# Streaming the folded w_in of a fused attention and two-MoE kernel past the packed values of all batches

## The chip, the cores and the metric

The kernel runs on one core of one Trainium2 chip. The metric is device time in microseconds (us): the median over the runs that are shown. Engines are called by name: TensorE (PE in the profile, PEld its weight loads), VectorE (DVE), ScalarE (ACT), GpSimd (POOL), SyncE (SP, which only issues DMAs here).

## The reference

```python
# q, k, v: (8 batches, 8 heads, 576, 64); p: (8, 8, 32, 64)
def sm_attn(qq, kk, vv):
    s = scale * np.matmul(qq, kk.transpose(0, 1, 3, 2))
    s = s - np.max(s, axis=-1, keepdims=True)
    a = np.exp(s)
    a = a / (np.sum(a, axis=-1, keepdims=True) + 1e-09)
    return np.matmul(a, vv)
p_packed = sm_attn(p, k, v)              # 32 packed rows for each head
out = sm_attn(q, p_packed, p_packed)
# heads side by side: x is (4608 tokens, 512)
def moe(x, w_in, w_out):                 # w_in (512, 2048), w_out (2048, 512)
    h = x @ w_in
    return (h * np.cos(h)) @ w_out
def moe2(x, w_in, w_out, a, b):          # the same sizes, g a ratio of polynomials in h
    ...
    return (g @ w_out).astype(np.float32)
```

The MoE weights arrive as 64-bit floats.

## The kernel before

**Precision.** A matmul of float32 accuracy is made of three matmuls on values that are split in a high part, rounded to the format that TensorE takes (F32R), and a low part, the rest: high x high, high x low, low x high (`PASSES`). `split` (lines 65 to 67) makes the high part with a copy on ScalarE and the low part with a subtraction on VectorE or GpSimd, as its caller says. `convert` (lines 74 to 93) turns a 64-bit weight chunk of 128 x 512 into the two parts: four operations on VectorE, three on ScalarE, two on GpSimd.

**W'.** The second attention ends in a product with p_packed and is followed by the product with w_in of the first MoE. The kernel multiplies p_packed by w_in first. For each batch this is W', 8 heads x 32 rows = 256 rows of 2048 columns, kept as two groups (`G`) of 128 rows. Then h = a W', where a is the second attention's softmax.

**First stage.** A loop over n = 0 to 16 (lines 386 to 412), one step for each batch and group of four heads, packs p: scores (`s1`), exponential, transposes (`et`), product with v (`pv`), transpose and split of the packed p (`ppt`). In its first steps three chunks of w_in a step are converted (line 402), all of w_in is kept in SBUF as high and low parts, and the second attention of batch 0 (`attn2_steps`) goes along, a step at a time. As soon as two batches (a pair P) are packed, the 16 units of their W' join a list, and each step works off four. A unit (`wunit`, lines 267 to 292) is three matmuls of 512 columns, a copy from PSUM (on ScalarE, every fourth on VectorE) into a tile `wev`, of which there are three, and, after every second unit, two stores to HBM of 256 KB each, issued by ScalarE.

**Between the stages.** A loop over the 16 chunks of w_out (lines 574 to 583) converts them, works off the last 16 units, and loads W' of batch 0 back (`load_wq`, four tiles of 512 columns) and splits it, the low part on GpSimd.

**First MoE.** 128 slots (`slots`, line 593), for 8 batches x 2 halves of the tokens x 8 pairs of blocks of 128 hidden columns. A slot makes h with 12 matmuls (`mm_h`), then the chain to g = h cos(h) (`chain1`), then, two slots late, y with 24 matmuls (`mm_y`, the sum over the pairs stays in PSUM). Two buffers in PSUM hold h. The chain reduces h to a cosine's range: ScalarE makes h/(2 pi) + 1/4, VectorE rounds it to a whole number and takes 2 pi times that from h, ScalarE takes the sine, VectorE multiplies by h. Between a batch's slots stand the next batch's second attention (every second slot), its loads and splits of W', and the conversions of the second MoE's weights (one in three slots, from slot 16 on).

**Second MoE.** 144 slots of 512 tokens x 128 hidden columns, 24 matmuls of 512 columns each.

**Order.** The program is written out without loops at run time. The framework orders each engine's instructions by the program's order and its own model of when they are ready, and adds the semaphores; each engine works off its queue in order. `hold` fixes single places of that order.

Of the kernel before, what the change touches and what calls it, by code (L numbers as in the profile page):

```python
# [20 lines left out]
def pack_attention_moe_moe_kernel(  # L21
# [76 lines left out]
    wd = [dram.tile([G, 128, DFF], F32, name=f"wd{b}") for b in range(B)]  # L98
# [11 lines left out]
    if True:  # L110
# [5 lines left out]
        e0, e0a = ExitStack(), ExitStack()  # L116
# [3 lines left out]
        ps0 = e0.enter_context(tc.tile_pool(name="ps0", bufs=1, space=PSUM))  # L120

        w1i_s = [[wb_p.tile([128, DFF], F32R, tag="wb", bufs=8, name="w1i") for x in range(2)] for i in range(NKD)]
# [33 lines left out]
        nc.vector.memset(coef[:, 6:7], 0.25)  # L156
# [92 lines left out]
        def ppt(n):  # L249
            b, g = divmod(n, G)  # L250
            P, b2 = divmod(b, 2)
            if P not in wl_t:
                wl_t[P] = tuple(
                    wi_p.tile([128, H // 2, 2, 64], F32R, tag=f"wl{i}", bufs=2, name=f"wl{i}") for i in range(2)
                )
# [9 lines left out]
        wev_t = {}  # L265

        def wunit(P, hp, fq):
            ps = ps0.tile([128, 512], F32, tag="w", bufs=2, name="w")
            wl = wl_t[P]
            for i, (a, c) in enumerate(PASSES):  # L270
                nc.tensor.matmul(  # L271
                    out=ps,
                    lhsT=wl[a][:, hp].rearrange("p b m -> p (b m)"),
                    rhs=w1i_s[hp][c][:, 512 * fq:512 * fq + 512],
                    start=(i == 0),
                    stop=(i == 2),
                )
            if fq % 2 == 0:
                wev_t[P, hp] = wi_p.tile([128, 1024], F32, tag="wev", bufs=3, name="wev")
            o = wev_t[P, hp][:, 512 * (fq % 2):512 * (fq % 2) + 512]  # L280
            if fq % 4 == 3:
                nc.vector.tensor_copy(o, ps)
            else:
                nc.scalar.activation(out=o, in_=ps, func=AF.Copy)
            if fq % 2 == 1:
                t = wev_t.pop((P, hp))
                g, gg = divmod(hp, 2)
                for b2 in range(2):
                    nc.scalar.dma_start(
                        out=wd[2 * P + b2][g, 64 * gg:64 * gg + 64, 512 * (fq - 1):512 * (fq + 1)],  # L290
                        in_=t[64 * b2:64 * b2 + 64, :],
                    )

# [3 lines left out]
        def attn2_steps(b, pool, psp, pst, psb, tg, now):  # L297
# [14 lines left out]
            for g in range(G):  # L312
# [12 lines left out]
                sc = psp.tile([128, 2, 512], F32, tag=pst, bufs=psb, name="s2")  # L325
# [17 lines left out]
            for g in range(G):  # L343
# [7 lines left out]
                split(ah, al, aT.rearrange("p c j -> p (c j)"), nc.gpsimd)  # L351
# [14 lines left out]
        cv1 = [(i, j) for i in range(NKD) for j in range(DFF // 512)]  # L366

        def load_w1i(x):
            i, j = cv1[x]
            load_st(x, words(w1i[128 * i:128 * i + 128, 512 * j:512 * j + 512]))  # L370

        def conv_w1i(x):
            i, j = cv1[x]
            c = slice(512 * j, 512 * j + 512)
            convert(w1i_s[i][0][:, c], w1i_s[i][1][:, c], st_t.pop(x), cv_p, 512)
            if x + 2 < len(cv1):
                load_w1i(x + 2)

        prep(0)
        load_w1i(0)  # L380
        load_w1i(1)

        units = []
        tg0 = {"qT": ("kT", 2), "ppT": ("pbd", 2), "aT": ("E", 2)}
        at = attn2_steps(0, wk, ps0, "s1", 1, tg0, lambda: None)
        for n in range(NG + 1):
# [8 lines left out]
            for _ in range(2):  # L395
                if units:
                    wunit(*units.pop(0))
# [7 lines left out]
            for _ in range(2):  # L405
                if units:
                    wunit(*units.pop(0))
# [356 lines left out]
```

## Time and profile before

| | |
|---|---|
| median of 3 runs | 1711.96 us (1711.77 to 1714.64) |
| profiled execution | 1713.67 us |
| its span, first to last instruction | 1711.9 us |
| mean granted clock of TensorE, share of full speed | 0.979 |
| TensorE, weight loads, VectorE, ScalarE, GpSimd busy | 94%, 82%, 81%, 68%, 17% |
| moved by DMA | 183.52 MB |

A row of the profile's lines view reads: line, engine, operation, what is written `<-` what is read (names of tiles), shapes, count | busy time in us, mean ns of one | idle time of the engine just before them, and what ended it. Shapes are partitions x elements. A line can be that of a helper: L67 is the low part of every `split`. Matmuls are pipelined, so TensorE's busy time is not that of an engine at its peak. "Xq" is the sequencer of engine X.

### The profile page before, as it was taken

Reading aid. Unit: us, or ns where it says so; the run is one execution under the profiler, and the core shown is the slowest. Engines: PE = TensorE matmul, PEld = TensorE weight load, DVE = VectorE, ACT = ScalarE, POOL = GpSimd, SP = SyncE. Lnnn points to the kernel's source line nnn. Section 1 sums busy time; section 2 is a strip of 40 time slices with the busy share of each in tenths; the row PEclk is TensorE's granted clock in tenths of the full one; section 3 lists DMA queues with packets and bytes.
Section 4 is the critical chain, followed back from the end, with each engine's and each line's share of the span. In section 5 each row is a group of like instructions: output and inputs, shape, how many; then the busy total and the mean of one; then the engine's idle time right before and its main releaser. Section 6 shows DMA issues by size and latency. Waiting matters only on the chain.

```text
span 1711.9 us, 24200 instructions
## 1 busy us (share of the span) xinstructions
PE 1614.5 (94%) x8832; PEld 1412.0 (82%) x8832; DVE 1382.4 (81%) x2143; ACT 1155.9 (68%) x1885; POOL 298.0 (17%) x203
## 2 busy tenths in 40 slices
PE   5789678999999999999999999999999999999996
PEld 4668478999999999999998888888888888888884
DVE  5893598888888888888658888888888888888884
ACT  3554566565656575756548777877777878787874
POOL 3450552233333332323100000000000000000000
PEclk9989889999999999999999999999999999999998
DMA  9988832443434433434285101001010202020100
GB/s 273 272 254 236 281 104 83 128 135 119 154 122 143 149 135 128 150 120 155 74 274 200 50 25 50 25 27 48 13 62 1 75 0 75 0 74 1 43 7 25
DMA packets 99767, 183.52 MB, mean 107 GB/s; under 512 B 11584, under 2 KB 46400, under 8 KB 99648
## 3 DMA queue, kind: packets, MB, share of 16 engines
q1 hardware_dynamic: 92224, 163.09, 30.0%
q10 hardware_dynamic: 7424, 18.88, 3.7%
q8 instruction: 70, 1.15, 0.3%
q14 instruction: 49, 0.40, 0.1%
HBM read 117.97 MB, written 63.96 MB: 106 GB/s over the span
## 4 chain that ended last, share of the span: by engine, by line
PE 74%; DVE 15%; ACT 4%; issue 3%; DMA 3%; SPq 0%; POOL 0%; ACTq 0%; DVEq 0%; POOLq 0%
PE h L643 23%; PE o L702 23%; PE y L558 14%; PE h L514 7%; PE s L191 3%; DVE gl L67 2%; DVE u L539 2%; DVE g L545 2%; DVE cvp L87 2%; PE w L271 1%; DVE cvp L89 1%; DVE r L540 1%; PE pv L237 1%; DVE cvf L90 1%; DMA st<-in_moe_w_in_dram 1%
## 5 line engine op out<-in xcount | busy, mean ns | idle before, releaser
L558 PE MATMUL y<-gh,w1o 128*128 128x288 f32 x2048 | 433.4, 297 | 0.0
L643 PE MATMUL h<-x,w 128*128 128x512 f32 x1728 | 422.7, 393 | 0.0
L643 PEld LDWEIGHTS h<-x,w 128*128 128x128 f32 x1728 | 324.1, 188 | 74.2
L558 PEld LDWEIGHTS y<-gh,w1o 128*128 128x128 f32 x2048 | 337.9, 189 | 1.4 <-DVE yl L67 0.7
L702 PE MATMUL o<-w,g2h 128*128 128x512 f32 x1152 | 334.0, 394 | 1.3 <-ACT g2h L661 1.3
L558 PE MATMUL y<-gl,w1o 128*128 128x288 f32 x1024 | 298.2, 297 | 8.1 <-DVE gl L67 7.9
L702 PEld LDWEIGHTS o<-w,g2h 128*128 128x128 f32 x1152 | 216.0, 188 | 53.1 <-ACT g2h L661 2.1
L514 PE MATMUL h<-ah,wq 128*128 128x288 f32 x1024 | 232.2, 303 | 26.9 <-DVE g L545 24.9
L558 PEld LDWEIGHTS y<-gl,w1o 128*128 128x128 f32 x1024 | 193.4, 189 | 11.7 <-DVE gl L67 11.3
L514 PEld LDWEIGHTS h<-ah,wq 128*128 128x128 f32 x1024 | 175.2, 192 | 30.4 <-issue 27.4
L702 PE MATMUL o<-w,g2l 128*128 128x512 f32 x576 | 199.8, 393 | 0.0
L677 ACT ACTIVATE sq<-h 128x512 f32<-128x512 f32 x144 | 87.3, 606 | 156.0 <-PE h L643 155.9
L679 DVE SCALAR_TENSOR_TENSOR ab<-sq,coef,ab 128x512 f32<-128x512 f32 x144 | 108.2, 751 | 68.1 <-ACT ab L678 67.9
L514 PE MATMUL h<-al,wq 128*128 128x288 f32 x512 | 153.5, 300 | 0.0
L544 ACT ACTIVATE r<-r,coef 128x576 f32<-128x576 f32 x128 | 99.0, 775 | 70.9 <-DVE r L540 70.1
L538 ACT ACTIVATE u<-h,coef 128x576 f32<-128x576 f32 x128 | 94.2, 736 | 76.1 <-PE h L514 75.4
L91 POOL TENSOR_TENSOR cvf<-cvf,cvs 128x512 f32<-128x512 f32 x64 | 89.6, 1400 | 288.7 <-DVE cvf L90 259.2
L688 DVE SCALAR_TENSOR_TENSOR ab<-ab,y 128x512 f32<-128x512 f32 x144 | 99.5, 691 | 47.8 <-ACT y L685 47.2
L67 DVE TENSOR_TENSOR gl<-g,gh 128x576 fp32r<-128x576 f32 x128 | 117.1, 917 | 18.2 <-ACT gh L66 16.1
L702 PEld LDWEIGHTS o<-w,g2l 128*128 128x128 f32 x576 | 108.0, 188 | 25.6
L680 ACT ACTIVATE c<-h,coef 128x512 f32<-128x512 f32 x144 | 113.8, 790 | 9.8 <-DVE g2l L667 9.8
L545 DVE TENSOR_TENSOR g<-h,r 128x576 f32<-128x576 f32 x128 | 95.9, 750 | 27.4 <-ACT r L544 27.3
(89 smaller groups left out, 2620.7 us busy)
## 6 DMA issues: line engine op xcount, KB each, us to landing
x<-yd SPq DMA_DIRECT2D x36, 512.0 KB
w<-w2d SPq DMA_DIRECT2D x68, 256.0 KB
st<-in_moe_w_in_dram SPq DMA_DIRECT2D x32, 512.0 KB
wd<-wev ACTq DMA_DIRECT2D x64, 256.0 KB
st<-in_moe_w_out_dram SPq DMA_DIRECT2D x32, 512.0 KB
wq<-wd SPq DMA_DIRECT2D x32, 512.0 KB
kx<-in_k_dram SPq DMA_DIRECT2D x16, 576.0 KB
vx<-in_v_dram SPq DMA_DIRECT2D x48, 192.0 KB
```

The costliest lines, as they stand in the source:

```text
L67: lo_eng.tensor_tensor(out=lo, in0=src, in1=hi.bitcast(F32), op=ALU.subtract)
L91: nc.gpsimd.tensor_tensor(out=ff, in0=ff, in1=sg, op=ALU.mult)
L514: last_h[0] = nc.tensor.matmul(out=ps[:, u, 0:HS], lhsT=wq[:, g, a, o:o + 128], rhs=a_t[b, g][c][:, hf * HS:hf * HS + HS], start=(i == 0), ...
L538: nc.scalar.activation(out=u, in_=ph, func=AF.Identity, scale=INV2PI, bias=coef[:, 6:7])
L544: nc.scalar.activation(out=r, in_=r, func=AF.Sin, bias=coef[:, 7:8])
L545: nc.vector.tensor_tensor(out=gt, in0=ph, in1=r, op=ALU.mult)
L558: nc.tensor.matmul(out=y_t[d][:, 0:HS], lhsT=w1o_s[f // 4][a][:, f % 4, 128 * d:128 * d + 128], rhs=gs[c][:, u], start=(f == 0 and i == 0) ...
L643: nc.tensor.matmul(out=ps, lhsT=w2_s[f][:, 0, a, 128 * kk:128 * kk + 128], rhs=x_t[t, c, kk], start=(i == 0), stop=(i == 3 * NKD - 1),)
L679: nc.vector.scalar_tensor_tensor(out=ab, in0=sq, scalar=coef[:, 5:6], in1=ab, op0=ALU.mult, op1=ALU.add)
L680: nc.scalar.activation(out=c1, in_=ph, func=AF.Identity, scale=coef[:, 3:4], bias=coef[:, 2:3])
L688: nc.vector.scalar_tensor_tensor(out=ab, in0=ab, scalar=QC, in1=y0, op0=ALU.add, op1=ALU.mult)
L702: nc.tensor.matmul(out=o_t[s], lhsT=g2_t[n][a][:, 128 * s:128 * s + 128], rhs=w2_s[f][:, 1, c], start=(f == 0 and i == 0), stop=(f == NFC ...
```

## The change

The first stage packs p of all batches and converts w_out (one chunk a step, two in two of the steps) and the first three chunks of w_in. W' is made afterwards: w_in streams through a ring of three chunks of 128 x 512, ordered by column block (`fq`, four of them) and then by head pair (`hp`, four). For each chunk `wunit(x)` makes one unit for each of the four pairs of batches; the unit's copy multiplies by 1/(2 pi) (three on ScalarE, one on VectorE), into one of two tiles `wev` of two units each, with two stores for each tile. When a column block is stored, its tile of W' for batch 0 is loaded back. From the second column block on, `slot` runs the first MoE's slots 0 to 5 between the chunks, one after every second chunk, with one PSUM buffer for h; slots 6 and 7 follow, and from slot 8 on there are two buffers again. The second attention of batch 1 has its eight steps in slots 8 to 15, one in each; later batches are as before.

W' and so h come scaled by 1/(2 pi). `chain1` now takes h as it comes: ScalarE adds a constant that rounds h to a whole number, VectorE subtracts constant and h, ScalarE takes the absolute value and then the sine, VectorE multiplies by 2 pi h. The low parts of W' and of the second attention are made on VectorE. Some tiles change pools and sides of SBUF.

```diff
-    wd = [dram.tile([G, 128, DFF], F32, name=f"wd{b}") for b in range(B)]
+    NQ = DFF // 512
+    NP = B // 2
+    wd = [dram.tile([B, G, 128, 512], F32, name=f"wd{i}") for i in range(NQ)]
...
-        nc.vector.memset(coef[:, 6:7], 0.25)
+        nc.vector.memset(coef[:, 6:7], RND)
...
+        def wunit(x):
+            fq, hp = cv1[x]
+            wi = w1i_t.pop(x)
+            g, gg = divmod(hp, 2)
+            dst = wd[fq].rearrange("(c b) g p f -> b g p c f", b=2)
+            for P in range(NP):
+                if P % 2 == 0:
+                    t = wi_p.tile([128, 2, 512], F32, tag="wev", bufs=2, name="wev")
+                ps = psw.tile([128, 512], F32, tag="w", bufs=2, name="w")
+                wl = wl_t[P]
+                for i, (a, c) in enumerate(PASSES):
+                    nc.tensor.matmul(
+                        out=ps,
+                        lhsT=wl[a][:, hp].rearrange("p b m -> p (b m)"),
+                        rhs=wi[c],
+                        start=(i == 0),
+                        stop=(i == 2),
                     )
 
+                if P == 2:
+                    nc.vector.tensor_scalar(out=t[:, P % 2], in0=ps, scalar1=INV2PI, scalar2=None, op0=ALU.mult)
+                else:
+                    nc.scalar.activation(out=t[:, P % 2], in_=ps, func=AF.Copy, scale=INV2PI)
+                if P % 2 == 1:
+                    for b2 in range(2):
+                        nc.scalar.dma_start(
+                            out=dst[b2, g, 64 * gg:64 * gg + 64, P - 1:P + 1], in_=t[64 * b2:64 * b2 + 64]
+                        )
...
-                split(ah, al, aT.rearrange("p c j -> p (c j)"), nc.gpsimd)
+                split(ah, al, aT.rearrange("p c j -> p (c j)"), nc.vector)
...
+        cvs = [(load_w1o, conv_w1o, f) for f in range(NFC)] + [(load_w1i, conv_w1i, x) for x in range(len(cv1))]
+        def conv_next():
+            i = at_cv[0]
+            at_cv[0] += 1
+            if i < len(cvs):
+                cvs[i][1](cvs[i][2])
+            if i + 2 < len(cvs):
+                cvs[i + 2][0](cvs[i + 2][2])
...
-            for x in range(3 * n, 3 * n + 3):
-                if 0 <= x < len(cv1):
-                    conv_w1i(x)
-            for _ in range(2):
-                if units:
-                    wunit(*units.pop(0))
+            conv_next()
+            if n in (5, 10):
+                conv_next()
...
-            nc.scalar.activation(out=u, in_=ph, func=AF.Identity, scale=INV2PI, bias=coef[:, 6:7])
-            nc.vector.tensor_scalar(out=u, in0=u, scalar1=RND, scalar2=RND, op0=ALU.add, op1=ALU.subtract)
+            nc.scalar.activation(out=u, in_=ph, func=AF.Identity, bias=coef[:, 6:7])
             nc.vector.scalar_tensor_tensor(
-                out=r, in0=u, scalar=-2.0 * math.pi, in1=ph, op0=ALU.mult, op1=ALU.add
+                out=r, in0=u, scalar=RND, in1=ph, op0=ALU.subtract, op1=ALU.subtract
             )
             finish_g(n - 1)
-            nc.scalar.activation(out=r, in_=r, func=AF.Sin, bias=coef[:, 7:8])
-            nc.vector.tensor_tensor(out=gt, in0=ph, in1=r, op=ALU.mult)
+            nc.scalar.activation(out=r, in_=r, func=AF.Abs)
+            nc.scalar.activation(out=r, in_=r, func=AF.Sin, scale=-2.0 * math.pi, bias=coef[:, 7:8])
+            nc.vector.scalar_tensor_tensor(
+                out=gt, in0=ph, scalar=2.0 * math.pi, in1=r, op0=ALU.mult, op1=ALU.mult
+            )
...
-        for f in range(NFC):
-            if f % 4 == 0:
-                for _ in range(4):
-                    wunit(*units.pop(0))
-                load_wq(0, f // 4)
-            conv_w1o(f)
-            if f + 2 < NFC:
-                load_w1o(f + 2)
-            if f % 4 == 2:
-                split_wq(0, f // 4, nc.gpsimd)
...
-                if s == 0:
-                    at = attn2_steps(b + 1, at_p, psh, "h", 2, {"aT": ("qT", 1)}, lambda: last_h[0])
-                if s % 2 == 1:
+                if s == (0 if b else 8):
+                    at = attn2_steps(b + 1, at_p, h_tile, {"aT": ("qT", 1)}, lambda: last_h[0])
+                if s % 2 == 1 if b else s >= 8:
                     next(at, 1)
...
-                        split_wq(b + 1, jj, nc.gpsimd, last_h[0])
+                        split_wq(b + 1, jj, nc.vector, last_h[0])
             if b > 0 and s == 0:
-                split_wq(b, 3, nc.gpsimd, last_h[0])
+                split_wq(b, 3, nc.vector, last_h[0])
             move_in(n)
...
+        for x in range(len(cv1)):
+            fq, hp = cv1[x]
+            wunit(x)
+            conv_next()
+            if hp == NKD - 1:
+                load_wq(0, fq)
+            if fq > 0:
+                if hp == 0:
+                    split_wq(0, fq - 1, nc.vector)
+                if hp % 2 == 1:
+                    slot(2 * (fq - 1) + hp // 2)
+        split_wq(0, NQ - 1, nc.vector)
+        for n in range(2 * NQ - 2, 2 * NQ):
+            slot(n)
```

## Rows read from the trace of the kernel before

**Rows 1.** Page, part 1: TensorE's busy us (share of span) and matmuls.

```profile
PE 1614.5 (94%) x8832; PEld 1412.0 (82%) x8832; DVE 1382.4 (81%) x2143; ACT 1155.9 (68%) x1885; POOL 298.0 (17%) x203
```

**Rows 2.** Window view, whole span in five stretches (columns: see prediction).

```profile
0.00:163.00 163.00, 128.87 (x555) 101.66 (x556) 117.31 (x243) 78.25 (x160) 63.54 (x63) 0.94 0.91 260
163.00:205.00 42.00, 30.20 (x106) 20.34 (x105) 17.19 (x29) 22.02 (x39) 18.46 (x11) 0.88 0.87 276
205.00:262.00 57.00, 38.31 (x248) 36.74 (x246) 54.79 (x74) 34.05 (x54) 30.04 (x22) 0.83 0.43 132
262.00:892.00 630.00, 613.41 (x4447) 601.76 (x4448) 530.57 (x788) 390.68 (x584) 185.93 (x109) 0.99 0.42 137
892.00:1712.00 820.00, 803.71 (x3483) 651.50 (x3482) 662.55 (x1012) 630.93 (x1049) 0.00 (x0) 0.99 0.13 44
```

**Rows 3.** Wait view, 163 to 262 us: total us, times, longest.

```profile
POOL wq L67 <- DMA wd<-wev: 35.5, 1, 35.5
```

**Rows 4.** Wait view, 262 to 892 us: total us, times, longest.

```profile
PE h L514 <- DVE g L545: 14.4, 9, 6.0
PEld y L558 <- DVE gl L67: 11.3, 14, 2.7
```

**Rows 5.** Chain of waits, in order of time: start us, us, what.

```profile
8.52 9.59 DMA st<-in_moe_w_in_dram
...
131.25 1.94 PE s L191 x8
...
147.63 1.94 PE s L191 x8
...
163.96 5.93 DMA wd<-wev
...
843.11 3.18 PE y L558 x24
```

**Rows 6.** Window view of line 514 (h matmuls): length, busy us (count), weight loads.

```profile
163.00:262.00 99.00, 17.69 (x97) 16.50 (x97) 0.85 0.62 193
```

**Rows 7.** Window view of line 558 (y matmuls), same columns.

```profile
163.00:262.00 99.00, 20.89 (x144) 19.99 (x144) 0.85 0.62 193
```

**Rows 8.** Lines, 0 to 163 us: one VectorE operation of a conversion.

```profile
L89 DVE TENSOR_TENSOR cvp<-st,cvp 128x512 f32<-128x512 uint32 x18 | 16.6, 920 | 0.2
```

**Rows 9.** Lines, whole span, forms apart, ScalarE: busy us, mean ns | idle before.

```profile
L538 ACT ACTIVATE u<-h,coef 128x576 f32<-128x576 f32 x128 | 94.2, 736 | 76.1 <-PE h L514 75.4
L544 ACT ACTIVATE r<-r,coef 128x576 f32<-128x576 f32 x128 | 99.0, 775 | 70.9 <-DVE r L540 70.1 <-DVE cvf L82 0.2
L66 ACT ACTIVATE gh<-g 128x576 fp32r<-128x576 f32 x128 | 86.9, 680 | 45.6 <-DVE g L545 44.8
L80 ACT ACTIVATE cvs<-st 128x512 f32<-128x512 f32 x64 | 42.7, 667 | 35.4 <-DMA st<-in_moe_w_in_dram 27.3 <-DMA st<-in_moe_w_out_dram 6.9 <-issue 1.2
L88 ACT ACTIVATE cvf<-cvf 128x512 f32<-128x512 f32 x64 | 40.2, 628 | 34.1 <-DVE cvp L87 32.6 <-DVE sm L215 0.9 <-ACT eT L228 0.5
L284 ACT ACTIVATE wev<-w 128x512 f32<-128x512 f32 x48 | 27.6, 593 | 21.4 <-PE w L271 14.4 <-DMA wd<-wev 5.7 <-PE et L226 1.2
```

**Rows 10.** Tile gl, 262 to 892 us, VectorE: ns min/median/max.

```profile
L67 DVE TENSOR_TENSOR gl<-g,gh x122: 716/757/2492, 262.7 to 890.6; 128x576 fp32r<-128x576 f32 x122
```

**Rows 11.** Page, part 6: DMA issues, engine, count, KB each.

```profile
wd<-wev ACTq DMA_DIRECT2D x64, 256.0 KB
st<-in_moe_w_in_dram SPq DMA_DIRECT2D x32, 512.0 KB
```

**Rows 12.** Tile wev, ScalarE's issues of W' stores: ns min/median/max.

```profile
L289 ACTq DMA_DIRECT2D wd<-wev x64: 452/453/1442, 56.5 to 210.1; - x64
```

**Rows 13.** Lines, 262 to 892 us, forms apart: VectorE and GpSimd.

```profile
L539 DVE TENSOR_SCALAR u<-u 128x576 f32<-128x576 f32 x120 | 70.2, 585 | 23.2 <-ACT u L538 22.9
L67 POOL TENSOR_TENSOR wq<-wq 128x1024 fp32r<-128x1024 f32 x27 | 68.6, 2539 | 71.9 <-ACT wq L66 71.9
```

More of the change, by code (lines that the diff above doesn't have):

```diff
@@ L119, in pack_attention_moe_moe_kernel @@
         wk = e0a.enter_context(tc.tile_pool(name="work0k", bufs=1))
-        ps0 = e0.enter_context(tc.tile_pool(name="ps0", bufs=1, space=PSUM))
-        w1i_s = [[wb_p.tile([128, DFF], F32R, tag="wb", bufs=8, name="w1i") for x in range(2)] for i in range(NKD)]
+        psw = e0.enter_context(tc.tile_pool(name="psw", bufs=1, space=PSUM, side="right"))
+        ps0 = e0p.enter_context(tc.tile_pool(name="ps0", bufs=1, space=PSUM))
         kx_t, vx_t = {}, {}
@@ L253, in ppt @@
                 wl_t[P] = tuple(
-                    wi_p.tile([128, H // 2, 2, 64], F32R, tag=f"wl{i}", bufs=2, name=f"wl{i}") for i in range(2)
+                    wi_p.tile([128, H // 2, 2, 64], F32R, tag=f"wl{i}", bufs=NP, name=f"wl{i}") for i in range(2)
                 )
@@ L263, in ppt @@
                 split(wlh[:, hp, b2], wll[:, hp, b2], ps[:, gg, 64 * gg:64 * gg + 64], nc.vector)
[L265 to L291, printed above, removed]
-                    )
@@ L295, in pack_attention_moe_moe_kernel, with attn2_steps @@
         a_t = {}
-        def attn2_steps(b, pool, psp, pst, psb, tg, now):
+        def attn2_steps(b, pool, new_ps, tg, now):
             def load(g):
@@ L324, in attn2_steps @@
                 yield
-                sc = psp.tile([128, 2, 512], F32, tag=pst, bufs=psb, name="s2")
+                sc = new_ps("s2")
                 scores(sc, ppT.rearrange("p e h m -> p e (h m)"), qT.rearrange("p e c j -> p e (c j)"))
@@ L440, in split_wq @@
             split(t[:, :, 0, :], t[:, :, 1, :], t[:, :, 1, :].bitcast(F32), eng, until)
-        def conv_w1o(f):
-            if f % 4 == 0:
-                w1o_s[f // 4] = [wb_p.tile([128, 4, DM], F32R, tag="wb", bufs=8, name="w1o") for x in range(2)]
-            hi, lo = w1o_s[f // 4]
-            convert(hi[:, f % 4], lo[:, f % 4], st_t.pop(f), cv_p, 512)
         def load_w2(i):
@@ L506, in mm_h @@
             b, hf, j = slots[n]
-            ps = psh.tile([128, 2, 512], F32, tag="h", bufs=2, name="h")
+            ps = h_tile("h")
             wq = wq_t[b, j // 2]
@@ L616, in pack_attention_moe_moe_kernel @@
                     if s == ss:
-                        split_wq(b + 1, jj, nc.gpsimd, last_h[0])
+                        split_wq(b + 1, jj, nc.vector, last_h[0])
             if b > 0 and s == 0:
-                split_wq(b, 3, nc.gpsimd, last_h[0])
+                split_wq(b, 3, nc.vector, last_h[0])
             move_in(n)
+        for x in range(len(cv1)):
+            fq, hp = cv1[x]
+            wunit(x)
[10 more added lines that the diff above has]
+            slot(n)
+        e0.close()
+        at_p = e1t.enter_context(tc.tile_pool(name="at", bufs=1, side="right", **RW))
+        psh.append(ehp.enter_context(tc.tile_pool(name="pshb", bufs=1, space=PSUM, side="right", **RW)))
+        for n in range(2 * NQ, len(slots)):
+            slot(n)
         finish_g(len(slots) - 1)
```

79 lines of the change are left out of this document (40 added, 39 removed).

## The prediction

> **What bounds the kernel now.** I read the page first: TensorE is busy 94% of the span [rows 1]. An average over stages with different limits says little, so I cut the span with the window view into five stretches [rows 2]. Its columns are the length, busy time and instruction count of TensorE's matmuls and of its weight loads, then VectorE, ScalarE and GpSimd, then the granted clock, the DMA share and GB/s.
>
> From 892 us on (the second MoE, which the change leaves alone) TensorE is busy 804 of 820 us. From 262 to 892 (the first MoE in steady state) it is busy 613 of 630, at clock 0.99, with VectorE busy 84% and ScalarE 62%. Before that it is not the bound. Up to 163 us (the first attention) the DMA engines are 91% busy at 260 GB/s, and VectorE 72%; from 163 to 205 DMA holds at 276 GB/s while VectorE is at 41%; from 205 to 262 VectorE is busy 54.8 of 57 us. So the front is first a transfer stage and then a VectorE stage.
>
> The wait view names what the middle costs. For 35.5 us GpSimd, which works in order, stood at the first low part of W' until W' had gone to HBM and come back, and the conversions of w_out stood behind it [rows 3]; VectorE made up for that after 205. In the steady stretch TensorE's waits end on VectorE: 14.4 us for the end of a slot's chain, 11.3 us for a low part of g [rows 4].
>
> The steady stretch has a simple price. In the chain of waits 24 y matmuls take 3.18 us [rows 5], so the 36 matmuls of a slot (12 h, 24 y, all of 288 columns) take 36 x 3.18/24 = 4.77 us. At 262 us 97 h and 144 y matmuls are done [rows 6, 7]: 241/36 = 6.7 slots, so 121.3 remain: 578.6 us. Seven later batches have two score groups each, at 1.94 us [rows 5]: 27.2 us. Of the 630 us, 630 - 578.6 - 27.2 = 24 are lost.
>
> **The change, part by part.**
>
> *Attention.* W' units leave this stage, and one or two conversions a step replace three. By 163 us 18 conversions had run on VectorE [rows 8]; 19 must run in the new stage, so one is added, four operations of at most 0.92 us: 3.7. VectorE loses the copies of W' by 163 (a quarter of 36 units, 9 x 0.6 as ScalarE's copy [rows 9]: 5.4) and gains two low parts of attention 2 at 0.76 [rows 10]: 1.5. So 117.3 - 5.4 + 3.7 + 1.5 = 117.1 us. At its densest long share, 54.8/57 = 0.96, that is 122 us. The first weight chunk lands at 8.5 + 9.6 = 18.1 us [rows 5]; with VectorE nearly idle until then, the stage ends near 140 instead of 163. Below: bytes. 163 us x 260 GB/s = 42.4 MB, less 36 stores of W' at 0.26 MB, plus one chunk, is 33.5 MB, at 276 GB/s 121 us. Above: from 131.25 to 147.63 two steps took 16.4 us [rows 5]; 16 steps at 8.2 and the start make about 150.
>
> *The new stage: 16 chunks, 64 W' units, six early slots.* Four bounds.
> - Bytes: 64 stores of 0.26 MB, 11 chunks of 0.52 still to come, four W' loads of 0.52 [rows 11], 24.7 MB; at 276 GB/s 89 us.
> - ScalarE: per chunk three copies at 0.593, four store issues at 0.453, a conversion of 0.667 + 0.628 + about 0.63 [rows 9, 12]: 5.5 us; 13 with and three without a conversion give 82. Six slots at 0.736 + 0.775 + 0.680 and an Abs at about 0.68 (the Copy of the same shape) add 17, three high parts of W' 3: 103, if no issue runs beside a copy. If half of the 29 us of issues do, 88.
> - TensorE: six slots 28.6; 192 matmuls of 512 columns at 4.77/36 x 512/288 = 0.236, 45: 74 us. Not the bound.
> - The store ring: three tiles become two, of the same 4 KB a partition. A tile takes two copies and two issues (2.1 us) and can be written again when both stores have landed; the one landing on the chain took 5.93 us [rows 5]. 8.0 us with two in turn is 4.0 a tile, and 32 tiles take 129 us.
>
> A new wait is in none of them: three times ScalarE's high part of W' waits, in order, for a store and a load (up to 2 x 5.93 us), with the next chunk's copies and stores and the early slots' chains behind it, and VectorE's low part behind it in turn; a chunk stands between, 100/16 = 6.2 us, so up to 3 x 5.6 = 17 us, or nothing if each landing is half as long. It counts in the upper end.
>
> I take 100, near ScalarE's sum: the 5.93 belongs to a moment when four W' loads were in the queue too, which here come one in four chunks. The ends 89 and 129 stay in the range. So the stage ends at 240.
>
> *Its price by a page.* The Trainium skill's "DMA: Bandwidth & Descriptors", section "Anatomy of one DMA", gives a transfer about 2.0 us fixed, mostly the write's receipt, and its bytes at 436 GB/s (for GpSimd's queue; ours is ScalarE's). As an estimate from that page, 0.52 MB lands in 3.2 us, a tile comes round in 5.3, and 32 tiles take 85 us, so the ring would not bind; the row's 5.93 says 129. No row here shows 3.2.
>
> *The last round trip.* Slots 6 and 7 need the last W' chunk: store, load, high part on ScalarE, low part on VectorE. Until then TensorE has slot 5 and the y of slots 3 and 4, about 8 us. I charge 10 us (two landings like the 5.93 would make 14; 6 if each is half of that). So at 250 us h of slots 0 to 5 and y of 0 to 4 are done: 192/36 = 5.3 slots, 122.7 left: 585.3 us.
>
> *Steady state.* W' comes scaled by 1/(2 pi), so a slot loses one VectorE operation (70.2 us over the stretch [rows 13]) and gains an Abs on ScalarE (121 x 0.68 = 82). Low parts move from GpSimd: 28 of W' with 1024 columns (0.757 x 1024/576 = 1.35 each, 38) and 14 of attention (11). VectorE: 530.6 - 70.2 + 38 + 11 = 509, 81%. ScalarE: 391 + 82 = 473, 75%. What else VectorE gains: the low part of g has a median of 0.757 us but a longest of 2.49, and GpSimd's low part of W' a mean of 2.54 [rows 10, 13]: VectorE stands still while GpSimd works, and 68.6 us of that go. The Trainium skill's "SBUF — State Buffer", section "SBUF: two separate sides", calls the port pair of these two engines an exclusive lock for a whole instruction; the longest row agrees, and by the rule alone at most those 68.6 us come back, on an engine whose waits cost TensorE 25.
>
> Of the 24 us lost I keep 17, and add 3 because the second batch's attention is squeezed into slots 8 to 15, a step in each: 20. Bounds: 10 (the waits for VectorE halved and more) and 30 (ScalarE's longer part of the chain makes up for all). Scratch layout, pool sides and conv buffers cost nothing: the stores keep their bytes, and the w2 conversions stay in the same slots.
>
> **Sum.** 250 + 585.3 + 27.2 + 20 = 882.5 us against 892: 9.5 us less, and the second MoE is unchanged. The profiled execution, 1713.67 us beside a span of 1711.9, would be 1704; it lies 1.7 over the median 1711.96, so 1702.5 by that median, and 1703 is forecast.
>
> **The rivals.**
> - *The store ring paces the new stage* (slower). At 129 us it costs 29 more: +19.5, 1731. It decides from the point where the stage takes 109.5 us, a tile cycle of 6.8, a landing of 4.7 us, and full half-way at 1721. For it: 5.93 on the chain, and ScalarE, in order, would hold the early slots' chains behind a store that waits; one issue took up to 1.44 us [rows 12]. Against it: DMA is less loaded here than at 163.
> - *ScalarE takes over* in the slots. The chain keeps its hops, but Abs and Sin follow each other behind copies of W', and 75% is a mean. The stage at 103 and 28 us lost: +1.5, 1713.
> - *Stores land fast and the bytes set the stage* (89 us, 11 less): -20, 1692; with attention on its byte bound too, 1674. The page above would bring this; no row does.
> - *The early slots don't fill the gap*: if W' returns later than the two chunks between load and first slot, the six slots run after the stage. That is 28.6 us of TensorE, less some 8 in the round trip: +11, 1723.
>
> **How the numbers follow.** The forecast has 0.44 (0.40 faster, 0.04 within 0.2%), own range 1692 to 1711; short landings 0.12, faster; the ring 0.22 and late early slots 0.07, slower; ScalarE 0.15 (0.10 the same, 0.05 slower). So faster 0.52, same 0.14, slower 0.34; 0.2%, 3.4 us, is about what a measurement tells from no change. The range reaches from inside the short-landing case, 1684, to inside the ring's, 1729.
>
> **What would show it.** Right: the last pack near 140 us; the last W' store near 240; slots from then on every 4.77 us with fewer waits for VectorE; h matmuls of slot 6 near 250. The long durations of VectorE's low parts go, GpSimd's W' rows are gone. Wrong: copies of W' waiting for stores, ScalarE with over 6.8 us a chunk, TensorE idle for over 15 us ahead of slot 6, waits for ScalarE's Abs or Sin in place of those for VectorE.

## The result and the profile after

The changed kernel takes **1736.85 us** (median of 4 runs, 1735.28 to 1740.55) against 1711.87 for the kernel before in the same comparison: ratio **1.0146, 95% interval 1.0125 to 1.0167**, slower by 25 us. The forecast was 1703 with a range to 1729, so it missed in sign and range. The profiled execution took 1735.52 us, its span 1732.6, mean granted clock 0.978.

The page's part 1, against [rows 1]: the engines' work moved the way that was forecast (VectorE 51 us less, ScalarE 75 more, GpSimd 108 less), and the time still rose.

```profile
PE 1618.7 (93%) x8832; PEld 1411.7 (81%) x8832; DVE 1331.1 (77%) x2063; ACT 1230.7 (71%) x2013; POOL 190.0 (11%) x155
```

The window view in six stretches, columns as in [rows 2]:

```profile
0.00:155.00 155.00, 107.56 (x444) 82.81 (x445) 120.13 (x246) 69.37 (x142) 69.54 (x67) 0.91 0.80 228
155.00:165.00 10.00, 8.87 (x43) 6.73 (x41) 2.18 (x8) 3.70 (x10) 0.63 (x1) 1.00 0.08 28
165.00:285.00 120.00, 89.58 (x411) 70.29 (x411) 63.41 (x83) 64.48 (x109) 30.73 (x24) 0.87 0.72 203
285.00:335.00 50.00, 45.61 (x305) 43.76 (x305) 34.44 (x49) 32.24 (x46) 0.00 (x0) 0.94 0.29 101
335.00:915.00 580.00, 565.67 (x4148) 556.21 (x4149) 448.83 (x666) 429.52 (x660) 89.14 (x64) 1.00 0.43 142
915.00:1732.00 817.00, 801.39 (x3485) 651.95 (x3483) 662.12 (x1012) 631.35 (x1049) 0.00 (x0) 0.99 0.13 44
```

In the 120 us from 165 on no engine is full: TensorE 75%, VectorE 53%, ScalarE 54%, DMA 72%. The wait view of 155 to 285 us (total, times, longest) says what they do instead:

```profile
PEld w L278 <- ACT wev L289: 24.9, 18, 4.1
ACT wev L289 <- DMA wd<-wev: 18.0, 11, 3.1
ACT wq L66 <- DMA wq<-wd: 10.8, 3, 6.3
DVE wev L287 <- DMA wd<-wev: 10.8, 4, 5.3
```

Copies of W' wait for stores (18.0 and 10.8 us), and TensorE for the copies. The chain of waits runs through those stores and ends in the last round trip:

```profile
166.44 5.19 DMA wd<-wev
...
173.46 6.08 DMA wd<-wev
...
252.41 3.58 DMA wd<-wev
...
268.58 3.19 DMA wd<-wev
...
271.86 5.59 DMA wq<-wd
...
277.47 1.06 ACT wq L66
...
278.56 1.24 DVE wq L67
...
279.84 2.78 PE h L516 x10
...
286.63 3.23 PE h L516 x12
```

Two tiles' rows fix the stages' ends (ns min/median/max, then first and last start in us): the exponentials of the packing steps, and the low part of the packed p, the last thing a pack makes.

```profile
L211 ACT ACTIVATE E<-s,nb x16: 719/736/741, 17.1 to 155.0; 128x576 f32<-128x576 f32 x16
...
L67 DVE TENSOR_TENSOR wl<-pt,wl x32: 181/210/225, 31.3 to 165.3; 128x64 fp32r<-128x64 f32 x32
```

The last pack ends at 165, not near 140. For some of the kernels below the same marks were taken from each trace, counting 12 h matmuls to a slot in order of time (us from the start of the span; "second" is the first h matmul of the second MoE). The order can differ from the program's: in the changed kernel the seventh group of 12, at 270.6 us, is a later slot's, since the W' of slots 6 and 7 was split from 277.5 us on.

| kernel | last exponential | last pack | last W' copy | slot 0 | slot 8 | slot 16 | second | span |
|---|---|---|---|---|---|---|---|---|
| before | 159.0 | 172.2 | 207.7 | 204.6 | 262.0 | 305.3 | 892.2 | 1711.9 |
| after | 155.0 | 165.3 | 270.0 | 191.1 | 286.6 | 334.6 | 915.4 | 1732.6 |
| before, units held late | 152.9 | 161.1 | 242.0 | 238.6 | 295.5 | 339.5 | 926.5 | 1746.2 |
| after, early slots held | 149.8 | 160.1 | 255.7 | 255.4 | 304.0 | 350.6 | 930.7 | 1747.8 |
| after, three store tiles | 154.6 | 165.2 | 258.2 | 187.0 | 274.4 | 322.4 | 905.0 | 1722.1 |
| after, no w_out conversion | 135.2 | 145.5 | 248.3 | 171.5 | 264.6 | 312.6 | 894.6 | 1711.8 |
| scaled chain, low parts later | 155.6 | 168.8 | 203.7 | 202.0 | 255.9 | 298.7 | 882.2 | 1702.1 |

So the loss is made before slot 16: +29.3 us there. From slot 16 to the second MoE the changed kernel gains 6.1 us (580.8 against 586.9), in the second MoE 2.5.

### The profile page after: what moved, and what is told of

Its sections match the earlier page's. It is cut to its first block, busy times and chain, and to the rows that moved or that the text cites. A ratio compares the mean times of both kernels' runs of the same rounds, so it can differ in the third digit from the quotient of the medians.

```text
span 1732.6 us, 24018 instructions
## 1 busy us (share of the span) xinstructions
PE 1618.7 (93%) x8832; PEld 1411.7 (81%) x8832; DVE 1331.1 (77%) x2063; ACT 1230.7 (71%) x2013; POOL 190.0 (11%) x155
## 3 DMA queue, kind: packets, MB, share of 16 engines
q1 hardware_dynamic: 92224, 163.09, 29.3%
q10 hardware_dynamic: 11520, 18.88, 4.1%
## 4 chain that ended last, share of the span: by engine, by line
PE 72%; DVE 6%; ACT 6%; DMA 4%; issue 2%; ACTq 0%; POOL 0%; DVEq 0%; SPq 0%
PE h L665 23%; PE o L724 23%; PE y L563 15%; PE h L516 9%; DMA wd<-wev 2%; PE s L192 1%; DVE r L542 1%; DVE g L548 1%; DMA wq<-wd 1%; ACT r L546 1%; ACT r L547 1%; DVE gl L67 1%; DVE sT L346 1%; ACT wev L289 1%; ACT L547 1%
## 5 line engine op out<-in xcount | busy, mean ns | idle before, releaser
L548 DVE SCALAR_TENSOR_TENSOR g<-h,r 128x576 f32<-128x576 f32 x128 | 95.7, 752 | 76.8 <-ACT r L547 76.4
L516 PE MATMUL h<-al,wq 128*128 128x288 f32 x512 | 152.9, 299 | 0.0
L91 POOL TENSOR_TENSOR cvf<-cvf,cvs 128x512 f32<-128x512 f32 x64 | 85.4, 1334 | 533.8 <-DVE cvf L90 365.3
L67 DVE TENSOR_TENSOR gl<-g,gh 128x576 fp32r<-128x576 f32 x128 | 107.2, 840 | 20.4 <-ACT gh L66 19.3
L542 DVE SCALAR_TENSOR_TENSOR r<-u,h 128x576 f32<-128x576 f32 x128 | 95.1, 745 | 32.9 <-ACT u L541 32.4
```

The source lines that it names most:

```text
L67: lo_eng.tensor_tensor(out=lo, in0=src, in1=hi.bitcast(F32), op=ALU.subtract)
L516: last_h[0] = nc.tensor.matmul(out=ps[:, u, 0:HS], lhsT=wq[:, g, a, o:o + 128], rhs=a_t[b, g][c][:, hf * HS:hf * HS + HS], start=(i == 0), ...
L542: nc.vector.scalar_tensor_tensor(out=r, in0=u, scalar=RND, in1=ph, op0=ALU.subtract, op1=ALU.subtract)
L548: nc.vector.scalar_tensor_tensor(out=gt, in0=ph, scalar=2.0 * math.pi, in1=r, op0=ALU.mult, op1=ALU.mult)
```

## The experiments

**Theories.** A: W' units cost almost nothing inside the first stage and are paid for where they are put. B: the ring of two store tiles paces the new stage. C: the single buffer for h, ScalarE's issues, or the streaming of w_in do.

### The parts that don't move w_in, alone and together

In the kernel before: the scaled chain alone, the low parts on VectorE alone, both.

```diff
-            nc.scalar.activation(out=u, in_=ph, func=AF.Identity, scale=INV2PI, bias=coef[:, 6:7])
-            nc.vector.tensor_scalar(out=u, in0=u, scalar1=RND, scalar2=RND, op0=ALU.add, op1=ALU.subtract)
+            nc.scalar.activation(out=u, in_=ph, func=AF.Identity, bias=coef[:, 6:7])
...
+            nc.scalar.activation(out=r, in_=r, func=AF.Abs)
...
-                        split_wq(b + 1, jj, nc.gpsimd, last_h[0])
+                        split_wq(b + 1, jj, nc.vector, last_h[0])
```

> The kernel before with only the two small parts of the change: W' stored times 1/(2 pi) with the new chain (Abs on ScalarE, one operation less on VectorE), and the low parts of W' and of the second attention on VectorE. Streaming is left out. Theory A (the W' units cost nothing in the first stage, because that stage is paced by its packing steps and conversions; moved out, they are exposed): the loss lies in the streaming, so this kernel is faster than before by 8 to 15 us (1697 to 1704), from fewer waits for VectorE in the steady stretch. Rival B (the ring of two store tiles) and rival C (the single h buffer) say the same here. Rival D (ScalarE's longer chain costs the steady stretch what VectorE saves): within 4 us of before, or slower.

> The kernel before with W' stored times 1/(2 pi) and the chain with Abs on ScalarE, low parts left on GpSimd. If relief from GpSimd is what counts, within 2 us of before (1709 to 1713). If the operation taken off VectorE is what counts, 3 to 6 us faster (1705 to 1708).

> The kernel before with the low parts of W' and of the second attention on VectorE, and nothing else. If the steady stretch gained because VectorE no longer stands behind GpSimd's long operations, this part alone gives the whole 4 us that both parts gave: 1704 to 1708. If it is the operation that the scaled chain takes off VectorE that counts, this one is level or slower (1710 to 1714), since VectorE gets about 49 us of work more.

Measured: both 1706.67 us, ratio 0.9982 (0.9967 to 0.9997); the scaled chain alone 1707.95, 0.9982 (0.9970 to 0.9994); the low parts alone 1712.80, 1.0007 (0.9997 to 1.0017). The scaled chain is worth about 3 us, the low parts alone nothing that can be measured. Both together gained about 3 us, where 8 to 15 were expected from this kernel; the rival of "within 4 us" came true. They lose nothing, so the loss of the whole change comes from the streaming of w_in and what belongs to it: the new place of the units, the ring and the early slots. In single profiles the scaled chain gained ahead of slot 16 (300.2 us), where VectorE is full, and nothing after it (586.9); both parts reached slot 16 at 304.1 and took 580.9 from there.

### W' units late, w_in left as it was

First only the program's order was changed: all 64 units in the loop between the stages.

```diff
-            for _ in range(2):
-                if units:
-                    wunit(*units.pop(0))
...
-                for _ in range(4):
+                for _ in range(16):
                     wunit(*units.pop(0))
```

> The kernel before with one thing changed: the W' units of the first three pairs of batches wait until the first stage is over, as in the changed kernel, and all 64 run between the stages, 16 ahead of each load of W'. w_in stays whole in SBUF, three store tiles, two h buffers, the old chain. Theory A (the units cost the first stage nothing): the last exponential of the first stage starts within 6 us of before (159.0), and what 48 units take is added between the stages: 20 to 40 us slower, 1731 to 1751. If the units held up the first stage as the forecast had it (some 20 us), the stage ends near 140 and the time is within 12 us of before.

1712.88 us, 1.0006 (0.9994 to 1.0017). This was no test: the framework had put units back where their operands were ready. The view of its tile `wev` up to 163 us shows 34 of the 64 store issues there, as before:

```profile
L289 ACTq DMA_DIRECT2D wd<-wev x34: 452/462/622, 54.3 to 162.5; - x34
```

So the next kernel holds each unit behind the last transpose of the packed p:

```diff
+                if i == 0:
+                    hold(mm, last_pt[0])
```

> The kernel before with every W' unit held behind the last transpose of the packed p on TensorE's queue (what the one without a hold did not do: the framework put 34 of the 64 units back into the first stage). w_in stays resident, three store tiles, stores by ScalarE, pairs in their old order. Theory 'the units cost little where they were and are paid in full where they are put': the 36 units of the first stage come after 160 us, 36 x (0.593 + 0.453) = 38 us of ScalarE and 9.4 MB of stores; the first stage ends at most 4 us sooner, slot 0 starts near 235 to 245 in place of 204.6 and the time is 1742 to 1750. Rival 'the units have room between the stages too': within 5 us of 1712.

1748.39 us, 1.0196 (1.0181 to 1.0211), in the range that theory A gave. The window view of this kernel up to 163 us, and the row of its copies of W':

```profile
0.00:163.00 163.00, 115.40 (x476) 89.64 (x476) 115.72 (x240) 68.03 (x140) 62.01 (x63) 0.88 0.71 210
```

```profile
L286 ACT ACTIVATE wev<-w x48: 578/597/600, 161.0 to 242.0; 128x512 f32<-128x512 f32 x48
```

Against [rows 2] 50 GB/s have gone from the first stage. Its last exponential comes only 6.1 us sooner (152.9 against 159.0; at most 4 were expected), its last pack 11.1 (161.1 against 172.2). Behind it the 64 units take 81 us (161.0 to 242.0): from the last exponential to slot 0 it is 85.7 us, in the kernel before 45.6. Slot 16 starts 34.2 us later. So A is shown for the larger part. Not for all of it: in the kernel before the units' matmuls (`w`) do stand on the chain of waits, for 11.1% of the 132 us from 27 to 159. When they are gone, the conversions on VectorE (`cvp`, `cvf`) take their place on it. The two chains, 27 to 159 us before and 27 to 153 us here:

```profile
by line: PE s L191 16.2%; PE pv L237 12.6%; PE w L271 11.1%; issue 7.3%; PE et L226 6.7%; DMA st<-in_moe_w_in_dram 5.9%; DVE kT L177 3.8%; DMA kx<-in_k_dram 3.7%; DMA vx<-in_v_dram 3.5%; DVE cvp L87 3.5%; DVE cvf L90 3.4%; DVE cvf L82 2.6%;
```

```profile
by line: PE s L191 18.1%; issue 10.3%; DVE kT L177 7.8%; PE et L226 7.2%; DVE cvp L87 5.9%; DVE cvf L82 5.3%; PE pv L237 5.1%; DVE cvp L89 4.9%; DVE mx L205 4.6%; DMA st<-in_moe_w_out_dram 4.4%; DVE cvf L90 4.3%; ACT E L210 2.9%; DVE sT L34
```

### The store ring, and who issues the stores

Three store tiles (the space comes from the chain, `r = u`), then the stores issued by SyncE, with three tiles and with two:

```diff
-                    t = wi_p.tile([128, 2, 512], F32, tag="wev", bufs=2, name="wev")
+                    t = wi_p.tile([128, 2, 512], F32, tag="wev", bufs=3, name="wev")
...
-                        nc.scalar.dma_start(
+                        nc.sync.dma_start(
                             out=dst[b2, g, 64 * gg:64 * gg + 64, P - 1:P + 1], in_=t[64 * b2:64 * b2 + 64]
```

> The changed kernel with three tiles for the stores of W' where it has two; the room comes from letting the chain work in place (r is u), nothing else is changed. Rival B (each tile comes back only when its stores have landed, and that sets the new stage): ScalarE's and VectorE's waits for stores, 18 and 11 us there, go, and the time falls by 15 to 29 us, to 1708 to 1722. Theory A: the stage is set by ScalarE and the bytes nearly as tightly, less than 8 us (1729 to 1737). Rival C: no change.

> The changed kernel with three store tiles (1721.9 us), and W' stores issued by SyncE instead of ScalarE. Theory 'ScalarE sets the new stage once the ring doesn't' : with three tiles the stage went from the last pack's exponential at 154.6 to the last W' copy at 258 us, 104 us, which is ScalarE's sum with all 64 issues of 0.45 us in it (103). Taking 29 us of issues off, the stage takes about 78 (TensorE's 74 next), the last copy comes near 232 and the time is near 1698. Rival 'the stage waits for the chain of one chunk, load, conversion, units, store, whoever issues': 1720 to 1724, the last copy near 256.

> The changed kernel (1736.9 us) with its two store tiles, stores issued by SyncE. Theory 'ring first, ScalarE's issues behind it': a tile still comes round only when its stores have landed, so the waits for stores stay (ScalarE 18 us, VectorE 11) but the issues no longer delay what stands behind them: 1720 to 1730. Rival 'issues alone are the cost': 1707 or less. Rival 'landings alone': 1735 to 1738.

Three tiles: 1721.93 us, 1.0068 (1.0053 to 1.0083), 15 us of the 25 back; slot 16 comes 12.2 us sooner. The tile's idle times show it: waits for a store (total us, times), in the changed kernel and with three tiles:

```profile
  DMA wd<-wev: 28.8, 15
```

```profile
  DMA wd<-wev: 4.2, 3
```

With SyncE issuing, three tiles gave 1728.99 us, 1.0086 (1.0066 to 1.0105), and two 1735.30, 1.0117 (1.0102 to 1.0132; the changed kernel 1.0146); the kernel before was at 1715.1 in that comparison. No gain where the ring is wide enough, at most a small one where it isn't: with two tiles the time lies in the range of the rival of landings alone, the ratio (1732 us on the scale of the others) between it and the theory, and the tile's waits for a store fell to 16.8 us in 14 times. The theory that ScalarE's issues set the stage falls. In the chain of the kernel with three tiles and SyncE's stores, chunk loads and ScalarE, VectorE and TensorE take turns:

```profile
179.95 5.75 DMA st<-in_moe_w_in_dram
...
211.49 7.15 DMA st<-in_moe_w_in_dram
...
227.84 4.22 DMA wd<-wev
...
232.14 3.77 DMA wq<-wd
```

### The single buffer for h, eight conversions later, and three mends together

```diff
-        for n in range(2 * NQ - 2, 2 * NQ):
-            slot(n)
         e0.close()
...
+        for n in range(2 * NQ - 2, 2 * NQ):
+            slot(n)
...
-            conv_next()
-            if n in (5, 10):
+            if n < 11:
                 conv_next()
```

> The changed kernel with the second PSUM buffer for h from slot 6 on instead of slot 8: the pools of the W' stage are closed ahead of slots 6 and 7. Rival C (slots 6, 7 and 8 run one after the other at 7.3 us each, since h has one buffer until the chain has read it): 5 to 8 us less, 1729 to 1732. Theory A and rival B: under 3 us of change.

> The changed kernel with eight of the 16 conversions of w_out moved from the first stage into the new stage, one beside each of the first eight chunks; the first stage converts eight chunks of w_out and three of w_in. Theory A, in the form that VectorE's conversions pace the packing steps: the first stage ends 15 to 23 us sooner (139 to 147 us instead of 162), the new stage grows by less, and the time falls by 8 to 20 us, to 1717 to 1729. If the packing steps are paced by their own chain of waits, the first stage ends where it did, and the time stays or grows. Rival B: the new stage is set by the stores, so it starts sooner and the whole gain is kept.

> The changed kernel with three store tiles, the second h buffer from slot 6 on and eight conversions in the new stage, all together. If the three remove separate pieces of time, their gains add (14.9 + 2.4 + 4.7 = 22 us): about 1715. If the earlier end of the first stage was kept from paying by the ring of two tiles, more: 1708 to 1713. If they remove the same time, no better than three tiles alone: 1720 to 1723. Theory A: not under 1707, the kernel with the other parts alone, since 48 units still stand where they hold up the slots.

Two buffers for h before slots 6 and 7: 1734.40, 1.0139 (1.0124 to 1.0154). Slot 16 came 1.6 us sooner (333.0): the buffer is worth little. Why was not tested. Eight conversions of w_out later: 1732.18, 1.0130 (1.0111 to 1.0149); the last exponential came 10.3 us sooner (144.7), but the last W' copy at 269.4 as in the changed kernel: the time was given back in the new stage. All three mends: 1723.39, 1.0068 (1.0047 to 1.0089), no better than the third tile alone.

### What holds the first stage, and the new one

```diff
-            convert(hi[:, f % 4], lo[:, f % 4], st_t.pop(f), cv_p, 512)
+            up = st_t.pop(f)[:, :, 1].bitcast(F32)
+            for o in (hi, lo):
+                nc.gpsimd.tensor_tensor(out=o[:, f % 4], in0=up, in1=up, op=ALU.subtract)
```

> The changed kernel with the 16 conversions of w_out left out: the chunks are still loaded, but two operations on GpSimd write zeros in place of the nine of a conversion, so the first MoE's output is zero. Off VectorE go 16 x 3.3 = 53 us of the first stage's 120, off ScalarE 16 x 1.9 = 30. Theory 'the conversions stand in the way of the packing steps on VectorE's queue' (eight of them moved out ended the stage 10.3 us sooner): the last exponential falls from 155 to about 130 to 135, near the bytes' 121. Rival 'a packing step is a chain of its own': 148 or more. The time follows the last exponential to within 5 us.

```diff
-            wi = w1i_t.pop(x)
+            wi = w1i_t[x % RING]
...
-        cvs = [(load_w1o, conv_w1o, f) for f in range(NFC)] + [(load_w1i, conv_w1i, x) for x in range(len(cv1))]
+        cvs = [(load_w1o, conv_w1o, f) for f in range(NFC)] + [(load_w1i, conv_w1i, x) for x in range(RING)]
```

> The changed kernel with three store tiles (1721.9 us), with only the first three chunks of w_in loaded and converted and used for all 16 places, so W' is wrong from the fourth on. Off the new stage go 13 loads and 13 conversions (ScalarE 25 us, VectorE 43). Theory 'the stage is a loop from chunk to chunk, load into one of two staging tiles, conversion, units, none of which is full': it falls from 104 us (154.6 to 258.2) to TensorE's 75 to 80, last W' copy near 233, 1697. Rival 'the stores or the early slots pace it': 95 us or more, 1713 to 1722.

Without conversions of w_out: 1716.71 us, 1.0034 (1.0020 to 1.0048), 20 us less than the changed kernel, and the last exponential 19.8 us sooner:

```profile
L211 ACT ACTIVATE E<-s,nb x16: 733/740/741, 16.1 to 135.2; 128x576 f32<-128x576 f32 x16
```

Sixteen conversions, each 2.9 us of VectorE by the pages' totals ((1331.1 - 1284.4)/16), cost 19.8/16 = 1.24 us each. Even with VectorE's work in the stage cut by a third, 15 steps take 135.2 - 16.1 = 119 us, 7.9 each. The expected 130 to 135 was met at its edge. What holds the rest isn't settled by this kernel: its DMA engines move 262 GB/s up to 135 us, as much as in the first stage of the kernel before (260), so the bytes may hold it too.

```profile
0.00:135.00 135.00, 103.27 (x443) 81.79 (x444) 78.33 (x182) 42.30 (x93) 57.27 (x67) 0.89 0.86 262
```

Without the stream of w_in: 1707.93 us, 0.9992 (0.9978 to 1.0005), 14 us less than with three tiles alone. Of these, 7 to 8 us are in the first stage (last pack 157.1), and the new stage went from 93.0 us (last pack to last W' copy) to 88.1. So 13 loads and 13 conversions are worth 5 us in it; the rival is nearer. ScalarE still issued the stores here, and copies of W' still waited for stores, 10.8 us in six times. TensorE is busy 75 of the 88 us, and 93% from 200 us on (first row the stage, second its later part):

```profile
157.00:245.00 88.00, 75.05 (x361) 57.83 (x360) 26.12 (x36) 44.37 (x71) 0.00 (x0) 0.96 0.75 203
200.00:245.00 45.00, 41.84 (x224) 35.10 (x225) 15.47 (x21) 23.47 (x38) 0.00 (x0) 0.96 0.71 186
```

### The early slots

```diff
-                if hp % 2 == 1:
-                    slot(2 * (fq - 1) + hp // 2)
...
-        for n in range(2 * NQ - 2, 2 * NQ):
+        for n in range(2 * NQ):
...
+                        if n < 2 * NQ and i == 0:
+                            hold(last_h[0], last_w[0])
```

The first kernel lacks the last two lines (slots 0 to 5 come after the chunks), the second has this hold too.

> The changed kernel with slots 0 to 5 run after the last W' chunk in place of between the chunks. Theory 'the early slots fill gaps of TensorE': the stage ends at most 8 us sooner (ScalarE has 13 us less in it), and the six slots with one buffer for h, 7.3 to 8 us each, come after it: 30 to 40 us slower, near 1770. Rival 'the early slots delay the chunks as much as they save': within 10 us of 1737.

> The changed kernel (1736.9 us) with slots 0 to 7 held behind the last W' unit on TensorE's queue. Theory 'the early slots are the change's one gain in the front': the chunks go by at about 5.3 us as the held units of the kernel before did (81 us for 64 units), the stage ends near 255, and eight slots of 7.3 us with one buffer for h take until 314 (slot 8 at 286.6 in the changed kernel): 1755 to 1765. Rival 'the early slots delay the chunks by what they save': slot 8 within 6 us of 286.6, 1731 to 1743.

The first: 1728.68 us, 1.0109 (1.0088 to 1.0131), faster than the changed kernel, and against the theory; but again the framework drew the slots forward (slot 0 at 190.9 us, slot 4 at 248.3), so it is no test of the theory. It shows that the program's order matters here by some 6 to 8 us: the last W' copy came at 263.3 in place of 270.0. With the hold: 1754.46 us, 1.0265 (1.0234 to 1.0295). The stage is 9 us shorter (95.6), slot 8 comes at 304.0 (314 was expected), slot 16 16.0 us later (350.6). The early slots do fill gaps; without them the change would lose some 42 us.

### The two parts that gain, each where it gains

The kernel before with the scaled chain everywhere, and low parts on VectorE from batch 2 on:

```diff
-                split(ah, al, aT.rearrange("p c j -> p (c j)"), nc.gpsimd)
+                split(ah, al, aT.rearrange("p c j -> p (c j)"), nc.gpsimd if b < 2 else nc.vector)
...
-                        split_wq(b + 1, jj, nc.gpsimd, last_h[0])
+                        split_wq(b + 1, jj, nc.vector if b else nc.gpsimd, last_h[0])
```

> The kernel before with the scaled chain everywhere, and low parts on VectorE only for batches 2 to 7; up to slot 16 GpSimd makes them as before. The scaled chain alone reached slot 16 at 300.2 us (before 305.3) and lost nothing after; both parts alone took 580.9 us from slot 16 to the second MoE (before 586.9) and reached slot 16 at 304.1. Theory 'the two gains belong to different stages and add': span 300.2 + 580.9 + 819.8 = 1700.9, 1702 to 1703, ratio 0.9945. Rival 'they lie within the scatter of one profile': 1706 to 1708, ratio 0.997 to 0.998.

1703.22 us, **0.9958 (0.9944 to 0.9973)**: faster than both kernels, by 7 us against before. Slot 16 starts at 298.7, the stretch to the second MoE takes 583.5: the gain is mostly ahead of slot 16.

## Why the prediction was wrong

**The step that failed: the attention "ends near 140 instead of 163".** It divided VectorE's sum by the density of another stretch [rows 2]. The sum was right (117.1 forecast, 120.1 measured up to 155 us); the density was not: 120.1/155 = 0.78, nearer to what it had been before (117.3/163 = 0.72). Nor is the stage its bytes: with W' gone, GB/s fell from 260 to 228, and the end hardly moved. The chains of waits above show what was overlooked: a packing step passes through every engine, and conversions stand between the steps on VectorE's queue. Without the 16 of w_out the last exponential came 19.8 us sooner. The last pack came at 165.3 where 140 was forecast: 25 us, the bulk of the miss. By the same mark the kernel before was at 172.2, so 7 us were gained where the forecast had 23. The upper bound that was written down, 150 from the steps' own pace [rows 5], was the better reading, and still 15 short: it took 8.2 us from two late steps, and the 15 steps from 17.1 to 155.0 us took 9.2 each. What followed from it failed too: units that leave this stage free 6 to 11 us there, not 23. Held late in the kernel before they cost 34.2 us at slot 16.

**The miss in the prediction's own terms.** At the first h of the second MoE it is 915.4 - 882.5 = 32.9 us: 25.3 for the first stage, 4.7 for the new one, nothing for the round trip, about 5 back since more slots were done by then, and 8 for the time lost from there on (rounded).

**The new stage, 100 us: the size held, not the reason.** From last pack to last W' copy it took 104.7. The forecast took ScalarE's 103 as the bound; with three tiles, SyncE's issues (no gain) and the run without conversions (5 us) show that it wasn't; that 100 came so near is partly luck. **The ring rival** named 1731 and the slower sign, with the place right: the waits for stores are there, and a third tile gives back 12.2 us at slot 16. But it asked for a stage of 129 us behind a first stage of 140, and the ring is 12 of the 29 us lost at slot 16, so that its 1731 came near the time is luck too. The Trainium skill's "DMA: Bandwidth & Descriptors", section "Anatomy of one DMA", gave the prediction an estimate of 3.2 us a landing. The nine landings on the chain took 3.2 to 6.1 us: 4.4 to 6.1 up to 202 us, 3.2 to 3.6 from 241 us on, and 3.6 and 5.1 between, so the estimate holds only at the lower end. Nor did the long landing of [rows 5], 5.93, need the four loads of W' to which the prediction put it down: here two took 5.19 and 6.08 us before the first of these loads was issued at 185.1.

**The last round trip, 10 us: right.** From the last W' copy (270.0) to slot 6's h (279.8, but for two matmuls) are 9.8. By then 86 h and 144 y matmuls were done, 6.4 slots' worth where 5.3 were forecast; 12 of the h matmuls are those of a later slot that the framework put ahead of slot 6.

```profile
0.00:279.80 279.80, 16.16 (x86) 14.36 (x86) 0.90 0.75 215
0.00:279.80 279.80, 21.14 (x144) 20.14 (x144) 0.90 0.75 215
```

The first row is line 516 (h), the second line 563 (y). The new wait of ScalarE's high part of W' was there too: 10.8 us in three times, inside the 0 to 17.

**The layout "costs nothing": wrong by a small term.** Stores in pieces of half the length (11,520 packets on ScalarE's queue, before 7,424, the same 18.88 MB) take longer to issue, against [rows 12]:

```profile
L292 ACTq DMA_DIRECT2D wd<-wev x64: 582/616/1330, 122.7 to 271.2; - x64
```

64 x (0.616 - 0.453) = 10 us more of ScalarE's queue, though the runs with SyncE's stores say that this cost little.

**Steady state: right from slot 16 on, too small a term ahead of it.** 24 us lost were to become 20: 17 kept and 3 for the squeezed attention. At the prediction's own prices (4.77 us a slot, 1.94 a score group) 17 of the 580.8 us from slot 16 on are lost, as forecast, 6.1 less than before. But from 279.8 to slot 16, 8.3 slots and two score groups (43.4 us) took 54.8: 11 lost where 3 were charged. The single buffer for h is some 2 of them by the run with two buffers; whether the squeezed attention is the rest was not tested. In the later stretch (335 to 915 us) TensorE's waits on the low part of g fell from [rows 4], those for the chain's end rose a little (11.6 us, in the kernel before 8.0 from 305 us on):

```profile
PEld y L563 <- DVE gl L67: 1.2, 4, 0.4
PE h L516 <- DVE g L548: 11.6, 13, 1.8
```

Low parts alone gave nothing measurable. The Trainium skill's "SBUF — State Buffer", section "SBUF: two separate sides", calls the port pair of VectorE and GpSimd a lock; taking 68.6 us of GpSimd off it and putting the same low parts on VectorE bought no time that the medians show (1.0007), which is no test of the lock by itself.

**The balance at slot 16.** From the kernel before to the changed one by way of two others: units held late, +34.2; then all else of the change, with the early slots held, +11.1 (350.6 against 339.5); then the early slots, -16.0. These add up to the measured +29.3 by construction. What is tested is the middle term alone: the third tile gives back 12.2 in the changed kernel, near the 11.1. But the two kernels of that term differ in streaming, conversions, layout and chain too, and in single profiles the same first stage ended at anything from 149.8 to 158.2 us, so this is good to a few us at best. Nor is it the only way to share out the loss: the third tile (15 us) and leaving out the stream (14 us, more than half of it in the first stage) together bring the time to 1707.9, about that of the two small parts alone, with the units still late and the early slots in place.

**Left open:** what paces a packing step once the conversions are gone, and how the loss divides between the units' place and the stream. Why the new stage takes 88 us without the stream is open as well; TensorE's 75 busy us there are about the 74 that the forecast summed for it, and nothing else was found as full. A third staging tile for the chunks beside three store tiles had no room and wasn't tried. The 2.5 us in the second MoE are not explained.

## What to carry to other kernels

Work that sits in the gaps of a stage in which no engine is full is paid for where it is moved to, and the stage it leaves can get shorter by much less: here 6 to 11 us against 34 us lost. Take the pace of such a stage from the distance of its own steps, over all of them, not from a sum over an engine divided by another stretch's density; and look at the chain of waits for what stands next on it. A ring that is made smaller, even by one tile, is worked out with landing times and kept as a case, not as a rival's tail. And before an order is believed, read it in the trace: twice here the framework put moved work back where it had been.

## What was not expected of the hardware

A store issue on ScalarE took 0.616 us (median) where the same 256 KB go out in pieces of half the length, and 0.453 before; 64 issues of each; the median was 0.58 to 0.62 in the other kernels with the shorter pieces whose stores ScalarE issues. Store landings on one chain took from 6.1 us early in the stage to 3.2 late in it, though not evenly.
